# Interleaving row loads with DMA transposes on SyncE, with new scheduler estimates, in a fused attention and SwiGLU kernel

## The chip, the cores and the metric

The kernel runs on one core of a Trainium2 chip. The metric is device time in microseconds (us) of one execution. Each variant was run several times, and medians are given. One run of each was profiled. A span is the profiled execution from its first to its last instruction, some 2 us shorter than the run's time.

## The reference

```python
# q, k, v: (8, 8, 576, 64) batch, head, row, dim;  s: (8, 8, 576)
scores = q @ k.T / 8                       # causal
cum    = cumsum(max(s, 0))                 # decay along the rows
scores = where(causal, -1e9, scores + min(-(cum_i - cum_j), 0))
x      = softmax(scores) @ v               # -> (4608, 512), heads side by side
xn     = x / sqrt(mean(x * x) + 1e-6) * rms_g
out    = (silu(xn @ w_gate) * (xn @ w_val)) @ w_out     # 512 -> 1536 -> 512
```

## The kernel before

The 4608 rows of the feed-forward part are cut into nine chunks of 512. The attention of batch b+1 runs on TensorE in the gaps of chunk b's matmuls. For batches 2 to 7, SyncE's queue carries three kinds of work: 15 row loads of a batch (five each of k, q and v, 256 KB, the fifth of each half that), 15 DMA transposes (five each of K, Q and the normalised x), and 4 output writes per chunk.

The program gives every operation an engine, an estimated duration and a key. A list scheduler simulates the engines with these estimates and so fixes the order of each engine's instructions before anything runs. For SyncE it also holds back a transfer until the simulated transfers in flight are nearly done:

```python
# in Plan.schedule(): candidates e of an engine, r = earliest start
if o.dma and e == "sp":
    r = max(r, self.dma_free - 3.0)
...
begin = max(self.dma_free, s + o.us + o.lags[0])
self.dma_free = begin + o.dma
o.done = self.dma_free + o.lags[1]
```

The operations that the change touches (second argument of `dma_start`: SyncE's estimated issue time; `dma`: estimated transfer time; `lags`: estimated lead and landing time):

```python
def load_rows(dst, src, b, eng, key):
    for sc in range(NB):                                  # NB = 5 blocks of 128 rows
        n = 128 if sc < 4 else 64
        ops.append(I(eng, "dma_start", 0.88 if eng == "pool" else 0.4, key=key,
                     dma=1.28 * n / 128, lags=(1.2, 1.2 if b < 2 else 4.2), ...))

def prep_cast(b, which, key):                             # which: 0 = k, 1 = q
    for sc in range(NB):
        I("dve", "tensor_copy", 0.34, key=key + sc, out=dst[0:n, sc], in_=src[0:n, sc])
        I("sp", "dma_start_transpose", 1.27, key=key + sc, dma=0.65, lags=(0.5, 2.7), ...)

def ffn2(c, key, step):                                   # second matmul stage of a chunk
    for tb in range(4):
        ...                                               # 12 matmuls into one PSUM bank O
        o = nxt("osb", osb)                               # three buffers, in turn
        I("act", "activation", 0.6, ..., out=o, in_=O, func=AF.Copy, scale=0.5)
        I("sp", "dma_start", 0.4, key=key, dma=0.72, out=out[...], in_=o)
...
for c in range(NCH):                                      # chunk c, K = 36 * c
    ...                                                   # FFN1 of chunk c
    for w in range(2):
        prep_cast(b, w, K - 14)                           # b = c + 1
    ...
    n = b + 1                                             # loads of the batch after it
    for o in load_rows(k_nat, k, n, "sp", K + 16) + load_rows(q_nat, q, n, "sp", K + 16): ...
    lv = load_rows(v_nat[n % len(v_nat)], v, n, "sp", K + 16)
    ...
```

## Time and profile before

| | before |
|---|---|
| median of 4 runs | 376.86 us (375.39 to 378.92) |
| span of the profiled run | 373.1 us (a run of 374.8 us) |
| TensorE busy | 341.8 us, 92% |
| TensorE idle | 31.3 us |

The profile is cut from the last matmul of one chunk's second stage to that of the next. These are chunks 3 to 6 of the kernel before; the columns are start and end, length, busy time of each engine with its instructions, granted clock, DMA share and GB/s.

```profile
144.70:185.50 40.80, 37.96 (x352) 27.68 (x352) 30.62 (x56) 25.87 (x55) 15.46 (x24) 0.96 0.85 160
185.50:227.10 41.60, 36.77 (x253) 17.67 (x257) 28.72 (x56) 26.61 (x57) 14.22 (x23) 1.00 0.83 159
227.10:266.70 39.60, 36.62 (x252) 17.63 (x256) 29.26 (x55) 25.58 (x55) 14.07 (x21) 1.00 0.85 162
266.70:304.20 37.50, 36.43 (x253) 17.61 (x257) 23.98 (x48) 22.40 (x48) 8.11 (x16) 1.00 0.39 76
```

TensorE, the first busy column, needs 36.4 to 36.8 us of a chunk at full clock, and the chunks take up to 41.6.

### The profile page before, as it was taken

The page shows a single profiled execution, that of the slowest core. Times are in us where ns is not written, and L with a number is a line of the kernel's source. Part 1 is how long each engine was busy: PE and PEld are TensorE (multiplying, and loading weights), DVE is VectorE, ACT ScalarE, POOL GpSimd, SP SyncE. Part 2 cuts the span into 40 slices and gives each one's busy share as a digit, 9 for nine tenths or more (in the row PEclk, how much of TensorE's full clock was granted, in tenths as well). Part 3 has the DMA queues.
Part 4 walks back from the last instruction along what each step waited for, and adds up shares of the span by engine and source line. Part 5 has one row for each costly group of instructions (what it writes and reads, how often), then busy time and mean ns, then how long its engine had stood idle before and what let it go on. Part 6 is the DMA issues. An engine that isn't in the chain of part 4 may idle for free.

```text
span 373.1 us, 7766 instructions
## 1 busy us (share of the span) xinstructions
PE 341.8 (92%) x2907; PEld 207.6 (56%) x2934; DVE 251.6 (67%) x486; ACT 230.4 (62%) x469; POOL 127.8 (34%) x211
## 2 busy tenths in 40 slices
PE   3869999999999997999979799979999999999993
PEld 3558775788577864787435444444445444444441
DVE  6478946797937895588837893879388638806830
ACT  3959698888769825874767547863687533313321
POOL 8976452504361544134613370345123200000000
PEclk9999999999999999899999999999999999999999
DMA  8999997977985997699758986699650170020012
GB/s 125 215 226 208 193 184 164 162 176 153 200 192 116 190 179 132 179 156 198 133 128 183 198 151 115 167 203 174 114 148 2 30 149 0 0 87 29 0 43 78
DMA packets 138356, 51.13 MB, mean 137 GB/s; under 512 B 127300, under 2 KB 132936, under 8 KB 138312
## 3 DMA queue, kind: packets, MB, share of 16 engines
q1 hardware_dynamic: 131688, 41.13, 55.8%
q0 software_dynamic: 6624, 9.44, 14.4%
q8 instruction: 25, 0.41, 0.5%
q14 instruction: 19, 0.16, 0.2%
HBM read 38.16 MB, written 9.44 MB: 128 GB/s over the span
## 4 chain that ended last, share of the span: by engine, by line
PE 62%; DMA 12%; DVE 9%; POOL 5%; SPq 4%; ACT 3%; issue 3%; DVEq 0%; ACTq 0%; POOLq 0%
PE psc L373 9%; PE psb L373 8%; PE psd L373 8%; PE psg L373 8%; PE psh L373 7%; PE psa L373 7%; PE psf L373 7%; PE pse L373 6%; DMA v_nata<-in_v_dram 5%; SPq L356 4%; DVE Hs L356 2%; DMA QTb<-q_bf 2%; DMA out_dram<-osbb 2%; DMA q_nat<-in_q_dram 1%; DMA k_nat<-in_k_dram 1%
## 5 line engine op out<-in xcount | busy, mean ns | idle before, releaser
L373 PEld LDWEIGHTS <-wv_sb 128*128 128x128 bf16 x624 | 60.7, 98 | 39.5 <-issue 7.2
L373 PEld LDWEIGHTS <-wg_sb 128*128 128x128 bf16 x624 | 58.6, 98 | 32.5 <-issue 5.1
L373 PEld LDWEIGHTS <-Hs 128*128 128x128 bf16 x432 | 41.3, 98 | 49.9 <-DVE Hs L356 2.1
L356 POOL TENSOR_TENSOR vwb<-v_nata,wT 128x512 bf16<-128x512 f32 (+1 forms) x20 | 21.1, 1073 | 12.2 <-DMA v_nata<-in_v_dram 11.9
L356 POOL TENSOR_SCALAR_AFFINE_SELECT Ea<-Ea 128x512 bf16<-128x512 bf16 x8 | 5.1, 644 | 56.0 <-ACT Ea L356 56.0
L356 ACT ACTIVATE sq_scr<-x_blka 128x512 bf16<-128x512 bf16 x19 | 12.0, 632 | 15.9 <-DVE x_blka L356 15.6
L356 DVE CAST q_bf<-q_nat 128x512 bf16<-128x512 f32 (+1 forms) x30 | 18.4, 621 | 3.7 <-DMA q_nat<-in_q_dram 3.7
L373 PE MATMUL psf<-xnT,wv_sb 128*128 128x256 bf16 (+1 forms) x116 | 20.6, 313 | 0.2
L356 ACT ACTIVATE sq_scr<-x_blkb 128x512 bf16<-128x512 bf16 x20 | 12.6, 630 | 13.1 <-DVE x_blkb L356 12.6
L356 POOL TENSOR_TENSOR vwa<-v_nata,wT 128x512 bf16<-128x512 f32 (+1 forms) x15 | 16.2, 1094 | 9.5 <-DMA v_nata<-in_v_dram 9.3
L356 DVE CAST k_bf<-k_nat 128x512 bf16<-128x512 f32 (+1 forms) x30 | 15.1, 515 | 5.2 <-DMA k_nat<-in_k_dram 5.2
L373 PE MATMUL psc<-wout_sb,Hs 128*128 128x512 bf16 x69 | 17.0, 379 | 0.9 <-DVE Hs L356 0.7
L373 PE MATMUL psd<-xnT,wg_sb 128*128 128x256 bf16 (+1 forms) x95 | 17.5, 316 | 0.1
L373 PE MATMUL pse<-xnT,wg_sb 128*128 128x256 bf16 (+1 forms) x102 | 17.3, 304 | 0.1
L373 PE MATMUL psh<-wout_sb,Hs 128*128 128x512 bf16 x70 | 16.6, 379 | 0.5 <-DVE Hs L356 0.4
L373 PE MATMUL psg<-wout_sb,Hs 128*128 128x512 bf16 x70 | 16.6, 379 | 0.1
L356 ACT ACTIVATE sq_scr<-q_bf 128x1024 bf16<-128x1024 bf16 (+1 forms) x18 | 16.5, 916 | 0.2
L373 PE MATMUL psc<-xnT,wg_sb 128*128 128x256 bf16 (+1 forms) x83 | 14.9, 316 | 1.8 <-DVE xnT L356 1.5
L373 PE MATMUL psb<-xnT,wg_sb 128*128 128x256 bf16 (+1 forms) x95 | 16.3, 308 | 0.1
L356 ACT ACTIVATE sq_scr<-k_bf 128x1024 bf16<-128x1024 bf16 (+1 forms) x18 | 16.3, 908 | 0.0
L356 DVE SCALAR_TENSOR_TENSOR x_blkb<-x_blkb,alb,gB 128x512 bf16<-128x512 bf16 x15 | 12.1, 859 | 5.0 <-POOL alb L356 5.0
L373 PE MATMUL psa<-xnT,wv_sb 128*128 128x256 bf16 (+1 forms) x75 | 13.4, 311 | 1.9 <-DVE u_sbc L356 1.7
(456 smaller groups left out, 859.6 us busy)
## 6 DMA issues: line engine op xcount, KB each, us to landing
k_nat<-in_k_dram SPq DMA_DIRECT2D x24, 256.0 KB, 4.7
q_nat<-in_q_dram SPq DMA_DIRECT2D x24, 256.0 KB, 5.8
v_nata<-in_v_dram SPq DMA_DIRECT2D x24, 256.0 KB, 5.1
out_dram<-osba SPq DMA_DIRECT2D x12, 256.0 KB, 2.3
out_dram<-osbb SPq DMA_DIRECT2D x12, 256.0 KB, 2.4
out_dram<-osbc SPq DMA_DIRECT2D x12, 256.0 KB, 2.4
v_nata<-in_v_dram POOLq DMA_DIRECT2D x8, 256.0 KB, 11.0
wg_sb<-in_moe_w_gate_dram POOLq DMA_DIRECT2D x2, 768.0 KB, 12.9
```

The costliest lines, as they stand in the source:

```text
L356: o = R.add(eng, us, lambda: f(**{n: real(a) for n, a in kw.items()}), outs, ins, key=key, lat=LAT[eng], kind=kind, dma=dma, name=outs[0]. ...
L373: nc.tensor.matmul(out, lhsT=lhsT, rhs=rhs, start=st, stop=sp)
```

## The change

Its intent: row loads go between the transposes, block by block, as soon as a buffer row is free, so that data is on chip long before its cast. With it come new estimates for the scheduler, a new rule for holding SyncE's transfers back, and another order in batch 0. The diff, cut to its core:

```diff
+        sp_free = 0.0                                    # end of SyncE's own transfers
-                        r = max(r, self.dma_free - 3.0)
+                        r = max(r, sp_free - 2.0)
+                if e == "sp":
+                    sp_free = self.dma_free
...
+    def load_row(dst, src, b, sc, eng, key):             # one of the five rows
-   dma_start  0.4   dma=1.28 * n / 128   lags=(1.2, 1.2 if b < 2 else 4.2)
+   dma_start  0.45  dma=1.2 * n / 128    lags=(1.2, 1.2 if b < NRUN else MARGIN + 1.2)
...
-    def prep_cast(b, which, key):
+    def prep_cast(b, key):
         for sc in range(NB):
+            for src, dst, out in ((k_nat, k_bf, KT[b % 2]), (q_nat, q_bf, QT[b % 2])):
-   dma_start_transpose  1.27  lags=(0.5, 2.7)
+   dma_start_transpose  1.31  lags=(0.5, 0.9 + 0.6 * MARGIN)     # MARGIN = 3.0; x too
...
-            I("sp", "dma_start", 0.4, key=key, dma=0.72,         # output write
+            I("sp", "dma_start", 0.62, key=key, dma=0.75,
...
-            for o in load_rows(k_nat, ..., K + 16) + load_rows(q_nat, ..., K + 16):
-            lv = load_rows(v_nat[n % len(v_nat)], v, n, "sp", K + 16)
+            K2 = K - 14 + LEAD                                   # LEAD = 0.5
+            for sc in range(NB):
+                for dst, src in ((k_nat, k), (q_nat, q)):
+                    o = load_row(dst, src, n, sc, "sp", K2 + sc)
+            lv = [load_row(v_nat[...], v, n, sc, "sp", K2 + 6 + sc) for sc in range(NB)]
...
-                        prep_norm(b, w, i, K + 30)
+                        prep_norm(b, w, i, K + 20 + 2 * i)
... batch 0 ("the start"):
-            k2 = key + step * (HP * hf + HP + 1.5)
+            k2 = key + step * (HP * hf + HP + 1.5) - (3 if b == 0 and hf == 0 else 0)
-    vops = [prep_v(0, sc, "dve", -70) for sc in range(NB)]
+    vops = [prep_v(0, sc, "dve", -70 if sc < 2 else -62) for sc in range(NB)]
-    R.after(vops[2], norms[2])
+    R.after(vops[2], norms[3])
-    gp_ = small_bank()
+    gp_ = bank("g", 1)
```

Estimated transfer times of the loads issued by GpSimd become smaller as well (1.28 to 1.08 us, 4.0 to 3.95, 9.6 to 8.0, 8.9 to 7.8).

More of the change, by code (lines that the diff above doesn't have):

```diff
@@ L285 @@
     NRUN = 2
+    LEAD = 0.5
+    MARGIN = 3.0
     NTWO = 2
@@ L400, in load_runs @@
         p0 = KP * which
-        return I("pool", "dma_start", 0.8, key=key, dma=(4.0, 3.45)[b] * (h1 - h0) / 8, lags=(0.9, 1.3),
+        return I("pool", "dma_start", 0.8, key=key, dma=(3.95, 3.35)[b] * (h1 - h0) / 8, lags=(0.9, 1.3),
                  out=raw[b][p0 : p0 + KP, h0:h1, :, :].rearrange("p h c d -> p h (c d)"),
                  in_=(k, q)[which][b, h0:h1, :, :].rearrange("h (p c) d -> p h (c d)", c=KC))
-    def load_rows(dst, src, b, eng, key):
-        ops = []
-        for sc in range(NB):
-            n = 128 if sc < 4 else 64
-            ops.append(I(eng, "dma_start", 0.88 if eng == "pool" else 0.4, key=key,
-                         dma=1.28 * n / 128,
-                         lags=(1.2, 1.2 if b < 2 else 4.2),
-                         out=dst[0:n, sc], in_=src[b, :, sc * 128 : sc * 128 + n, :].rearrange(
-                             "h p d -> p h d")))
-        return ops
+    def load_row(dst, src, b, sc, eng, key):
+        n = 128 if sc < 4 else 64
+        return I(eng, "dma_start", 0.88 if eng == "pool" else 0.45, key=key, dma=(1.08 if eng == "pool" else 1.2) * n / 128,
+                 lags=(1.2, 1.2 if b < NRUN else MARGIN + 1.2), out=dst[0:n, sc],
+                 in_=src[b, :, sc * 128 : sc * 128 + n, :].rearrange("h p d -> p h d"))
+    def load_rows(dst, src, b, eng, key):
+        return [load_row(dst, src, b, sc, eng, key) for sc in range(NB)]
     def load_w(which, lo, hi, key):
         if which == 2:
-            return I("pool", "dma_start", 0.84, key=key, dma=9.6 * (hi - lo) / 12,
+            return I("pool", "dma_start", 0.84, key=key, dma=8.0 * (hi - lo) / 12,
                      out=wout_sb[:, lo:hi, :],
@@ L421, in load_w @@
         dst, src = ((wg_sb, moe_w_gate), (wv_sb, moe_w_val))[which]
-        return I("pool", "dma_start", 0.76, key=key, dma=8.9 * (hi - lo) / DF,
+        return I("pool", "dma_start", 0.76, key=key, dma=7.8 * (hi - lo) / DF,
                  out=dst[:, :, lo:hi],
@@ L438, in prep_transpose @@
             I("act", "activation", 0.57, key=key, out=o, in_=i, func=AF.Copy)
-    def prep_cast(b, which, key):
-        src, dst = ((k_nat, k_bf), (q_nat, q_bf))[which]
-        out = (KT, QT)[which][b % 2]
+    def prep_cast(b, key):
         for sc in range(NB):
             n = 128 if sc < 4 else 64
-            I("dve", "tensor_copy", 0.34, key=key + sc, out=dst[0:n, sc], in_=src[0:n, sc])
-            I("sp", "dma_start_transpose", 1.27, key=key + sc, dma=0.65, lags=(0.5, 2.7),
-              out=out[:, :, sc * 128 : sc * 128 + n], in_=dst[0:n, sc])
+            for src, dst, out in ((k_nat, k_bf, KT[b % 2]), (q_nat, q_bf, QT[b % 2])):
+                I("dve", "tensor_copy", 0.34, key=key + sc, out=dst[0:n, sc], in_=src[0:n, sc])
+                I("sp", "dma_start_transpose", 1.31, key=key + sc, dma=0.65,
+                  lags=(0.5, 0.9 + 0.6 * MARGIN),
+                  out=out[:, :, sc * 128 : sc * 128 + n], in_=dst[0:n, sc])
     def prep_norm(b, which, i, key):
@@ L613, in att_out @@
             c0 = b * S + tb * 128
-            I("sp", "dma_start_transpose", 1.27, key=key - 3, dma=0.65, lags=(0.5, 2.7),
+            I("sp", "dma_start_transpose", 1.31, key=key - 3, dma=0.65, lags=(0.5, 0.9 + 0.6 * MARGIN),
               out=xnT[:, :, c0 : c0 + 128 - p0], in_=x_blk[b % 2][p0:128, tb, :])
@@ L752 @@
             else:
-                for w in range(2):
-                    prep_cast(b, w, K - 14)
+                prep_cast(b, K - 14)
             if b < NRUN:
@@ L764 @@
             n = b + 1
-            for o in load_rows(k_nat, k, n, "sp", K + 16) + load_rows(q_nat, q, n, "sp", K + 16):
-                if n == NRUN:
-                    R.after(o, *vops)
-            lv = load_rows(v_nat[n % len(v_nat)], v, n, "sp", K + 16)
+            K2 = K - 14 + LEAD
+            for sc in range(NB):
+                for dst, src in ((k_nat, k), (q_nat, q)):
+                    o = load_row(dst, src, n, sc, "sp", K2 + sc)
+                    if n == NRUN:
+                        R.after(o, *vops)
+            lv = [load_row(v_nat[n % len(v_nat)], v, n, sc, "sp", K2 + 6 + sc) for sc in range(NB)]
             if n == NRUN:
```

## The prediction

> **What bounds the kernel now.** I read, in this order: the page's busy shares, then busy time by stretch, then SyncE's timeline, then the waits of TensorE and VectorE, then the first 30 us. The page says that TensorE is the engine to feed:
>
> ```profile
> PE 341.8 (92%) x2907; PEld 207.6 (56%) x2934; DVE 251.6 (67%) x486; ACT 230.4 (62%) x469; POOL 127.8 (34%) x211
> ```
>
> Of the 373.1 us span TensorE is idle for 31.3 us. 5.8 us of that lies before its first matmul and 5.1 us after its last (output and its landing); the change touches neither. What is left to win is 20.4 us. Where it lies, the stretches tell (length, then busy time of each engine, granted clock, DMA share, GB/s):
>
> ```profile
> core 0: us, PE busy (x) PEld busy (x) DVE busy (x) ACT busy (x) POOL busy (x), PEclk, DMA share, GB/s
> 120.00:160.00 40.00, 37.14 (x345) 26.86 (x344) 29.83 (x56) 26.30 (x57) 15.73 (x24) 0.96 0.86 162
> 160.00:199.60 39.60, 37.33 (x314) 23.28 (x315) 30.01 (x57) 26.22 (x56) 15.10 (x24) 1.00 0.87 160
> 199.60:239.20 39.60, 36.37 (x251) 17.55 (x255) 28.46 (x55) 25.42 (x54) 14.17 (x23) 1.00 0.86 162
> 239.20:279.00 39.80, 36.30 (x250) 17.35 (x253) 29.22 (x57) 25.57 (x55) 14.07 (x21) 1.00 0.84 161
> 64.00:120.00 56.00, 55.05 (x526) 41.30 (x527) 40.79 (x85) 44.46 (x95) 20.98 (x32) 1.00 0.84 171
> ```
>
> The four stretches from 120 to 279 us are one chunk of the feed-forward part each, with one batch of attention in it. TensorE idles 2.86 + 2.27 + 3.23 + 3.50 = 11.86 us in them, 7.5%. From 64 to 120 us, with the same kinds of work, it idles 0.95 us, 1.7%. Something holds the later chunks at 39.6 us. SyncE's timeline of one of them names it (start, time, what):
>
> ```profile
> 199.57 4.39 SPq L356 DMA_DIRECT2D k_nat<-in_k_dram  x5
> 204.01 6.49 SPq L356 DMA_DIRECT2D q_nat<-in_q_dram  x5
> 210.60 5.59 SPq L356 DMA_DIRECT2D v_nata<-in_v_dram  x5
> 216.28 2.57 SPq L356 DMA_TRANSPOSE xnT<-x_blkb  x2
> 218.94 1.22 SPq L356 DMA_TRANSPOSE KTa<-k_bf  x1
> ...
> 237.89 1.24 SPq L356 DMA_TRANSPOSE QTa<-q_bf  x1
> ```
>
> One piece begins where the last ended, from 199.57 to 239.18 us, where the next chunk's loads begin. Summed by kind over that chunk: 15 row loads 4.39 + 6.49 + 5.59 = 16.5 us, 15 transposes 18.6 us, 4 output writes 3.0 us; 38.0 us in all, and some 20 gaps make up the other 1.6 us. SyncE's queue is full, and its order is the pace of these chunks. The first load of a burst takes 0.57 us to issue, one in its middle 1.12 us: with several in flight SyncE is held to the rate at which they move. What TensorE feels of it:
>
> ```profile
> 149.27 0.27 PE L373 MATMUL psb<-QTa,KTa 64*128 64x256 bf16 x1 [2.21 <-DMA QTa<-q_bf]
> 189.48 0.27 PE L373 MATMUL psf<-QTb,KTb 64*128 64x256 bf16 x1 [1.62 <-DMA QTb<-q_bf]
> 209.73 0.66 DVE L356 CAST q_bf<-q_nat 128x512 bf16<-128x512 f32 x1 [1.51 <-DMA q_nat<-in_q_dram]
> 211.03 1.02 PE L373 MATMUL psa<-xnT,wv_sb 128*128 128x512 bf16 x4 [1.74 <-DVE u_sbc L356]
> ```
>
> Twice the scores wait for a transpose that came late. And VectorE, in order, sits before a cast whose q rows have not landed; the u product behind it in its queue is what TensorE then waits for (again at 250.93 us, 1.75 us). After the 2.21 us wait the clock fell as well:
>
> ```profile
> 144.00:152.00 8.00, 5.43 (x43) 3.56 (x41) 2.01 (x3) 2.84 (x6) 1.11 (x1) 0.91 0.59 131
> 152.00:160.00 8.00, 8.00 (x77) 6.51 (x76) 6.41 (x13) 7.45 (x18) 1.91 (x3) 0.88 0.59 158
> ```
>
> A mean of 0.91 and 0.88 over 8 us each is (0.09 + 0.12) x 8 = 1.7 us of clock lost, which counts as busy time. The start, last:
>
> ```profile
> 18.13 1.29 DVE L356 TENSOR_TENSOR vwa<-v_nata,psc 128x512 bf16<-128x512 f32 x2 [1.79 <-DMA v_nata<-in_v_dram]
> 20.62 0.43 PE L373 MATMUL psd<-vwa,Ee 128*128 128x65 bf16 x5 [2.30 <-DVE vwa L356]
> 26.15 1.03 PE L373 MATMUL psc<-xnT,wg_sb 128*128 128x256 bf16 x8 [1.51 <-DVE xnT L356]
> ```
>
> VectorE waits 1.79 us for v rows before it norms the last two head pairs of batch 0's first half, and the first feed-forward matmul starts at 26.15 us.
>
> **What the Trainium skill says.** "DMA: Bandwidth & Descriptors", section "Anatomy of one DMA": the DMA engines do not wait for semaphores; the wait is on the issuing sequencer. The timeline agrees: SyncE's issue order decides what starts, and a held issue holds all behind it. The same page, "Queues, rings and completion order": descriptors of one queue's ring are taken in order. So a transpose behind loads starts after them; here the first transpose after the v loads took 3.66 us from issue to landing against a median of 2.5 us. "TensorE: Matmul & The Clock Gate", Part 1: the clock is halved after an idle window of about 3.4 us. This trace fits only in part: 1.7 us lost is 3.4 us at half clock, but the wait before it was 2.2 us.
>
> **The change, part by part.** The instruction orders of both kernels were compared engine by engine. No operation is added or removed: TensorE has the same 1440 blocks of 512 columns of feed-forward work and the same attention work. What changes is order; the new durations and lags are only the scheduler's estimates.
>
> (1) Row loads. Before, SyncE issues 15 loads of a batch in a burst, shortly before that batch's casts and transposes. After, each pair of K and Q transposes of batch b is followed by the K and Q load of the same block of batch b+1, in the buffer rows that the casts have just freed; v loads come last in the chunk. So loads are almost a chunk ahead of their casts: the waits of VectorE on k and q rows and of GpSimd on v rows (21 us in all, 9 times) should go. Cost on SyncE: 15 transposes 18.6 us and 4 writes 2.5 us as before; 10 interleaved loads. A group of two transposes and two loads issues in 2 x 1.3 + 2 x 0.6 = 3.8 us; as an estimate from landing spacings (about 1.15 us for a load in a burst, 0.75 us for a transpose) it moves for 3.8 us. That is balanced, so a load will still be held at times: I take 0.75 us, 7.5 us for ten; the five v loads stay a burst, 5.6 us; gaps 1.6 us. Sum 18.6 + 2.5 + 7.5 + 5.6 + 1.6 = 35.8 us, where 39.6 us were needed. TensorE's 36.3 to 37.3 us become the longer of the two.
>
> (2) Places of the scores. In TensorE's order, counted in feed-forward blocks of 0.216 us, the first scores of batch 4 move from block 440 to 452, of batch 5 from 584 to 620, of batch 6 from 728 to 744; batch 7 stays at 872. Behind the third transpose pair they have 36 to 44 blocks, 7.8 to 9.5 us, against 2.6 us issue and 2.5 to 4 us landing. So the 2.21 and 1.62 us waits should go, and with the first the lost clock.
>
> Gain in the four chunks: 11.86 us idle + 1.7 us clock = 13.6 us at most. I keep 2.5% idle of 159 us, 4.0 us (1.7% is the rate of 64 to 120 us; some more because SyncE is at 35.8 us, and the wait of the second matmul stage for the last Hs, 0.4 to 0.7 us a chunk, does not depend on the loads). 13.6 - 4.0 = 9.6 us.
>
> (3) Batch 0. In VectorE's new order the v factors of blocks 3 and 4 still stand before the norms of pairs 2 and 3; only block 2's, 0.68 us, goes behind them and behind a square of 0.69 us. TensorE's transposes of x move ahead of half of the second half's matmuls. So the 1.79 us wait stays, and the second half starts later, at about 21.9 us for 20.62. The first feed-forward matmul should come at about 25.4 us, 0.7 us earlier. But batch 1's transposes now stand behind 52 feed-forward blocks for 60: TensorE reaches them at about 25.4 + 52 x 0.216 + 1.2 = 37.8 us, and q's first half landed at 39.7 us. A new wait of 1 to 2 us takes back the 0.7 us. Net 0, give or take 1.
>
> Sum: 377.0 - 9.6 + 0 = 367.4, say 367.5 us.
>
> **The rivals.** (A) SyncE stays the bound: if interleaved loads keep the 1.1 us of a burst, SyncE needs 18.6 + 2.5 + 11 + 5.6 + 1.6 = 39.3 us, and only the waits for q rows and the lost clock go, because data comes a chunk earlier: 371 to 374 us. For it speaks a DMA share of already 0.85, against it the 0.57 us of an issue with room. (B) Transposes stuck behind two loads in the ring land 1 to 2 us later, and scores wait for QT again, each with a chance of a halved clock: 370 to 375 us. For it speaks 3.66 us after a burst; against it the moved scores. (C) All idle time in the chunks falls to 1.7% or less and the start keeps its 0.7 us: 377.0 - 13.6 + 2.7 - 0.7 = 365.4; 362 if also the handovers inside chunks shrink. (D) Denser attention stretches (batch 5 in 78 blocks, before 88) make VectorE the bound there: some 1 us a chunk, 369 to 371 us.
>
> **Range and chances.** The 2% line is 369.5 us, so the middle lies only 2 us beyond it. C and the main line give faster (0.68); A, B and D, alone, mostly end between 369.5 and 375 (0.29); slower needs stalls that the old order did not have (0.03). Range 362 to 373 us.
>
> **What would show each step right or wrong.** Right: in SyncE's timeline loads of about 0.6 to 0.8 us between transposes, with waits for its producers; chunks of 37 to 38 us between 120 and 279 us; no wait of VectorE on k or q rows after 100 us, none of GpSimd on v rows; no scores waiting for QT over 1 us; clock 1.00 all through; first feed-forward matmul near 25.4 us and a wait for batch 1's q rows near 38 us. Wrong: chunks still near 39 us with SyncE without gaps (A), or waits of TensorE on QT (B) or on u and Hs products (D) in place of the old ones.

## The result

The changed kernel takes 360.71 us (median of 4 runs, 359.86 to 364.39) where the one before takes 376.86. The ratio is 0.9586, 95% interval 0.9507 to 0.9666: faster by 4.1%. A ratio here is the mean time of one kernel's fast runs over the mean time of the other's in the same rounds, so it is not quite the ratio of the medians. The prediction had said 367.5 us within 362 to 373: the direction was right, the size was not, and the result lies 1.3 us below the range. A later repeat gave 360.37 us, ratio 0.9592 (0.9547 to 0.9637).

The page's busy shares and the engines of the chain that ended last, of the changed kernel:

```profile
PE 339.0 (94%) x2934; PEld 206.7 (58%) x2934; DVE 247.0 (69%) x486; ACT 231.6 (65%) x469; POOL 126.5 (35%) x211
PE 78%; DMA 9%; POOL 6%; DVE 3%; issue 1%; ACT 1%; DVEq 0%; POOLq 0%; ACTq 0%
```

TensorE does the same work in 339.0 us (341.8 before), and idles 19.9 us of the span of 358.9, not 31.3. Before, TensorE had 62% of the chain and SyncE's queue 4%; SyncE has now left the list. Where the time went, chunk by chunk (lengths between the last matmuls of the second stages, in us; chunk 0 from the first feed-forward matmul on, which starts at 26.15 before and at 25.21 after):

| chunk | 0 | 1 | 2 | 3 | 4 | 5 | 6 | 7 | 8 |
|---|---|---|---|---|---|---|---|---|---|
| before | 42.3 | 38.1 | 38.2 | 40.8 | 41.5 | 39.7 | 37.4 | 31.5 | 31.1 |
| after | 43.2 | 37.5 | 38.1 | 36.1 | 36.1 | 37.7 | 35.9 | 31.5 | 31.1 |

The span shrank by 14.2 us, of which 4.7 + 5.4 + 2.0 + 1.5 = 13.6 us lie in chunks 3 to 6. (Medians differ by 16.1 us because the profiled run of before was 2.1 us below its median.) The same stretches of the changed kernel:

```profile
144.00:180.20 36.20, 36.20 (x354) 27.15 (x353) 29.79 (x61) 27.41 (x57) 13.75 (x23) 1.00 0.94 176
180.20:216.20 36.00, 35.99 (x257) 17.61 (x256) 26.38 (x50) 24.07 (x51) 14.62 (x23) 1.00 0.93 171
216.20:254.00 37.80, 36.39 (x258) 17.86 (x257) 29.91 (x58) 27.89 (x60) 13.91 (x22) 1.00 0.87 160
254.00:289.90 35.90, 35.90 (x258) 17.56 (x257) 23.84 (x48) 23.22 (x48) 8.12 (x16) 1.00 0.29 55
```

In three of the four TensorE has no idle time at all: 36.20 of 36.20, 35.99 of 36.00, 35.90 of 35.90. In chunk 5 it idles 1.4 us, in pieces of 0.2 to 0.7 us, each behind VectorE or GpSimd; none of these waits is on a transfer.

SyncE's timeline of the changed kernel (start, time, what), from the v loads of one chunk on:

```profile
159.38 4.98 SPq L361 DMA_DIRECT2D v_nata<-in_v_dram  x5
164.46 2.57 SPq L361 DMA_TRANSPOSE xnT<-x_blka  x2
167.12 1.98 SPq L361 DMA_TRANSPOSE KTb<-k_bf  x1
169.15 1.26 SPq L361 DMA_TRANSPOSE QTb<-q_bf  x1
170.46 0.58 SPq L361 DMA_DIRECT2D k_nat<-in_k_dram  x1
171.09 0.57 SPq L361 DMA_DIRECT2D q_nat<-in_q_dram  x1
171.76 1.49 SPq L361 DMA_TRANSPOSE KTb<-k_bf  x1
...
175.90 0.91 SPq L361 DMA_DIRECT2D out_dram<-osba  x1
```

The loads do sit in pairs between transposes, at 0.57 to 0.64 us each. But the queue is as full as ever. The next chunk's v loads start at 196.19, 36.81 us later. The pieces between are k and q loads 5.9 us, v loads 5.0, transposes 21.9, output writes 2.2, and gaps 1.9. The transposes cost 3.3 us more than before, because several are held where others take 1.2 to 1.3 us: three right behind a pair of loads (1.49, 1.54 and 1.67 us), one behind the v loads and two transposes (1.98), and two of x behind output writes (1.65 and 1.74).

One thing I had overlooked shows in the waits of ScalarE: who waited, for what, us in total, times, longest. Before:

```profile
ACT osbc L356 <- DMA out_dram<-osbc: 8.0, 2, 5.2
ACT osbb L356 <- DMA out_dram<-osbb: 5.0, 2, 2.6
ACT osba L356 <- DMA out_dram<-osba: 3.2, 1, 3.2
```

And after, the only such line of any output buffer:

```profile
ACT osbb L361 <- DMA out_dram<-osbb: 1.7, 1, 1.7
```

Before, an output write was issued late because it stood in SyncE's full queue: in chunks 2 to 5, 4 to 12 us after ScalarE had filled its buffer (ends of the copies set against the issues in the timeline). With three buffers, ScalarE then waited before the fourth copy of each of the chunks 1 to 5, 16.2 us in all, and held a PSUM bank meanwhile. TensorE itself waited for these copies only 0.5 us in all. After, writes of the same chunks are issued within 0 to 4 us.

The start: the wait behind the v factors is still there, as the prediction said.

```profile
21.52 0.31 PE L378 MATMUL psd<-vwa,Ee 128*128 128x65 bf16 x5 [2.52 <-DVE vwa L361]
```

### The profile page after: what moved, and what is told of

The parts are those of the page before. It is cut to its first block, busy times and chain, and to the rows that moved or that the text cites. A ratio compares the mean times of both kernels' runs of the same rounds, so it can differ in the third digit from the quotient of the medians.

```text
span 358.9 us, 7827 instructions
## 1 busy us (share of the span) xinstructions
PE 339.0 (94%) x2934; PEld 206.7 (58%) x2934; DVE 247.0 (69%) x486; ACT 231.6 (65%) x469; POOL 126.5 (35%) x211
## 4 chain that ended last, share of the span: by engine, by line
PE 78%; DMA 9%; POOL 6%; DVE 3%; issue 1%; ACT 1%; DVEq 0%; POOLq 0%; ACTq 0%
PE pse L378 12%; PE psa L378 10%; PE psh L378 10%; PE psb L378 10%; PE psf L378 9%; PE psd L378 9%; PE psc L378 9%; PE psg L378 8%; DMA wv_sb<-in_moe_w_val_dram 5%; DMA v_nata<-in_v_dram 4%; POOL v_nata L361 2%; POOL q_nat L361 1%; ACT sq_scr L361 1%; DVE Hs L361 1%; POOL Ee L361 1%
## 5 line engine op out<-in xcount | busy, mean ns | idle before, releaser
L378 PE MATMUL pse<-wout_sb,Hs 128*128 128x512 bf16 x96 | 22.5, 379 | 0.0
L361 ACT ACTIVATE sq_scr<-x_blka 128x512 bf16<-128x512 bf16 x19 | 12.0, 630 | 12.0 <-DVE x_blka L361 11.6
L378 PE MATMUL psc<-xnT,wg_sb 128*128 128x256 bf16 (+1 forms) x104 | 18.8, 316 | 0.0
L361 DVE SCALAR_TENSOR_TENSOR x_blkb<-x_blkb,alb,gB 128x512 bf16<-128x512 bf16 x15 | 11.0, 779 | 10.8 <-POOL alb L361 10.7
L378 PE MATMUL psa<-wout_sb,Hs 128*128 128x512 bf16 x72 | 17.0, 379 | 0.0
L378 PE MATMUL psb<-xnT,wv_sb 128*128 128x256 bf16 (+1 forms) x100 | 16.5, 302 | 0.2 <-DVE u_sbc L361 0.2
L361 DVE CAST q_bf<-q_nat 128x512 bf16<-128x512 f32 (+1 forms) x30 | 15.3, 510 | 0.9 <-ACT sq_scr L361 0.9
L378 PE MATMUL pse<-xnT,wg_sb 128*128 128x256 bf16 (+1 forms) x92 | 15.5, 305 | 0.0
L378 PE MATMUL psa<-xnT,wg_sb 128*128 128x256 bf16 (+1 forms) x84 | 15.5, 318 | 0.0
L361 POOL TENSOR_TENSOR vwa<-v_nata,wT 128x512 bf16<-128x512 f32 (+1 forms) x15 | 15.1, 1039 | 0.0
L361 DVE CAST k_bf<-k_nat 128x512 bf16<-128x512 f32 (+1 forms) x30 | 13.7, 456 | 0.0
```

The lines of the kernel that those rows point to most:

```text
L361: o = R.add(eng, us, lambda: f(**{n: real(a) for n, a in kw.items()}), outs, ins, key=key, lat=LAT[eng], kind=kind, dma=dma, name=outs[0]. ...
L378: nc.tensor.matmul(out, lhsT=lhsT, rhs=rhs, start=st, stop=sp)
```

## The experiments

All kernels gave correct results, and all 18 runs were timed in rounds with the kernel before on the same chip. The texts on record number the theories in the order in which they were formed: the first two credit the interleaving, the third the scheduler's new estimates, the fourth the late output writes alone, the last the pace of SyncE's issues.

### First set: the parts of the change, one at a time

**Interleaving alone.** The new load order and paired casts, with all old estimates and the old start:

```diff
-   load_rows(k_nat, ..., K + 16) + load_rows(q_nat, ..., K + 16);  v the same
+   load_row per block at K - 14 + 0.5 + sc;  v at K - 14 + 6.5 + sc
    (every duration, transfer time, lag and the hold-back rule as before)
```

> The kernel before with one part of the change: K and Q row loads of batch b+1 follow the two transposes of the same block of batch b, v loads last, casts of k and q alternate. The scheduler's estimates and the start of batch 0 stay as before. Theory 1 (SyncE's issue time is the pace of chunks 3 to 6, because a burst of loads is held to the rate of the transfers) and theory 2 (rows land too late for the in-order VectorE and GpSimd) both expect nearly all of the gain: about 363 us, chunks 3 to 6 near 36 to 37 us each. Theory 3 (the gain comes from later places of the scores in TensorE's order, set by the new lags) expects 373 us or more, with scores waiting for QT.

Measured: 382.03 us, ratio 1.0139 (1.0062 to 1.0216). It is slower than the kernel before. The waits for Q transposes and q rows are gone, just as planned, but TensorE now waits for ScalarE's copies, up to 6.26 us, and its mean granted clock falls to 0.976 (0.995 before). One such place, from the timelines of SyncE, ScalarE and TensorE of this kernel:

```profile
231.69 3.94 SPq L357 DMA_DIRECT2D v_nata<-in_v_dram  x4
235.72 1.10 SPq L357 DMA_DIRECT2D out_dram<-osbb  x1
240.14 0.60 ACT L357 ACTIVATE osbb<-psa 128x512 f32<-128x512 f32 x1 [8.59 <-DMA out_dram<-osbb]
240.79 1.86 PE L374 MATMUL psa<-xnT,wv_sb 128*128 128x512 bf16 x4 [6.26 <-ACT osbb L357]
```

The buffer osbb had been filled by 225.04 us, but SyncE gets to its write only at 235.72, behind k, q and four v loads. ScalarE waits 8.59 us to reuse the buffer, and TensorE 6.26 us for the PSUM bank that ScalarE could not empty. So the interleaving by itself relieves one wait and makes another, and the two theories that credit it alone, with 363 us, fall. The third had the time right (373 us or more) and the reason wrong: no scores wait for QT.

**New estimates alone.** Loads stay in a burst and the start stays old; all new issue and transfer times, the hold-back rule and the earlier key of the norms are in.

```diff
-   r = max(r, self.dma_free - 3.0)
+   r = max(r, sp_free - 2.0)
    (and 0.4 -> 0.45, 0.4 -> 0.62, 1.27 -> 1.31, MARGIN, prep_norm at K + 20 + 2 * i)
```

> The kernel before with only the scheduler's new durations, lags, load throttle and the earlier key of the norm squares; loads stay a burst of 15 behind the transposes, the start of batch 0 as before. Theories 1 and 2 expect within 1.5% of before: 371 to 379 us, with SyncE's queue still full at about 39 us a chunk. Theory 3 expects most of the gain, about 363 us.

Measured: 369.39 us, 0.9776 (0.9711 to 0.9841), about half of the gain, and between what the first two theories and the third expected. TensorE still waits 6.4 us for Q and K transposes and ScalarE 13.9 us for output writes.

**The start alone.**

```diff
-    R.after(vops[2], norms[2])
+    R.after(vops[2], norms[3])        (and the other three edits of batch 0)
```

> The kernel before with only the changes of batch 0: v factors of blocks 2 to 4 at a later key, block 2's after the fourth norm, the first half's squares and outputs 3 earlier, the small transposes of g in a bank group of its own. All theories expect the same as before, 375 to 378 us: the first feed-forward matmul 0.5 to 1 us earlier, and that lost again by the end of chunk 0, whose end in the two known profiles is 68.5 and 68.4 us.

Measured: 375.82 us, 0.9987 (0.9920 to 1.0054): nothing. The first feed-forward matmul comes at 25.00 us, 1.15 us earlier, yet chunk 0 ends at 68.7 us for 68.5.

**Everything but the start.**

```diff
-    R.after(vops[2], norms[3])
+    R.after(vops[2], norms[2])        (and the other three edits undone)
```

> The changed kernel without the changes of batch 0. All theories expect the time of the changed kernel within 1 us: 360 to 362 us.

Measured: 363.28 us, 0.9623 (0.9567 to 0.9679), 1.3 us above the expected range; the third set comes back to this.

Without the start, the four corners are 377.4 us (neither), 382.0 (interleaving), 369.4 (estimates) and 363.3 (both). Added up, the two single effects make +4.7 - 8.0 = -3.3 us; together they make -14.1. The other 10.8 us come only from having both.

### Second set: which estimates, and are the late writes the cause

**Interleaving plus SyncE's new issue and transfer times.** The hold-back rule is in too; the norms' key, GpSimd's estimates and the start stay old. Since the lags are the same in both kernels, the expectation's other branch could not come true; this kernel differs from "everything but the start" in the norms' key and GpSimd's estimates alone.

```diff
     on top of "interleaving alone":
-   r = max(r, self.dma_free - 3.0);  0.4 / 1.28 (load), 1.27 (transpose), 0.4 / 0.72 (write)
+   r = max(r, sp_free - 2.0);        0.45 / 1.2,        1.31,             0.62 / 0.75
```

> Interleaved loads alone (382.0 us) plus only the new issue and transfer costs on SyncE and the new load throttle; lags, key of the norm squares and batch 0 as before. In its order the output writes stand before the loads that stood before them in the run with interleaved loads alone. Theory 4 expects that to bring most of the fall: 362 to 367 us. If the added lags are what counts, it stays above 372 us.

Measured: 363.98 us, 0.9678 (0.9633 to 0.9723). A handful of constants takes the interleaved kernel from 382 to 364 us, nearly level with "everything but the start". ScalarE's waits for output writes fall from 21.9 to 0.7 us. SyncE's timeline shows where the writes now stand:

```profile
215.28 0.58 SPq L360 DMA_DIRECT2D q_nat<-in_q_dram  x1
215.96 0.83 SPq L360 DMA_DIRECT2D out_dram<-osbb  x1
216.88 0.38 SPq L360 DMA_DIRECT2D out_dram<-osbc  x1
```

They follow a pair of loads directly, 3 to 4 us after their copies started (211.80 and 213.89 us), with no v loads in between.

**The changed kernel with no slack in its landing lags.**

```diff
-    MARGIN = 3.0
+    MARGIN = 0.0
```

> The changed kernel with the added lag (3 us for loads, 1.8 us for transposes in the scheduler's estimate) set to 0, so scores and casts are placed closer behind their transfers. If the added slack is what the new estimates bring, it loses 4 us or more, with TensorE waiting for QT. If the issue costs and the load throttle are what they bring (so that SyncE's order of writes, loads and transposes fits the chip), it stays within 2 us of the changed kernel, 359 to 363 us.

Measured: 361.79 us, 0.9599 (0.9562 to 0.9637). The slack for late landings hardly matters.

**Output writes issued by ScalarE**, in the kernel before and in "interleaving alone", to take them out of SyncE's queue:

```diff
-            I("sp", "dma_start", 0.4, ..., out=out[...], in_=o)
+            ... nc.scalar.dma_start(out=out[...], in_=o)      (order as planned for SyncE)
```

> The kernel before with the output writes issued from ScalarE's queue; all other instructions keep their order. It takes about 3 us a chunk from SyncE's queue of 38 us. Theory 1 (SyncE's queue is the pace of chunks 3 to 6) expects 1.5 to 3 us a chunk, 366 to 371 us. Theory 3 (only places of scores) and theory 2 (rows late) expect less: rows are issued no earlier relative to their casts than SyncE's order allows, so 373 us or more if SyncE's total is not what counts.

> The kernel with interleaved loads alone (382.0 us), with the output writes issued from ScalarE's queue in place of SyncE's; every engine's other instructions keep their order. Theory 4, formed from that run's trace: interleaving does take the waits for rows and for QT away, but under the old estimates SyncE's order puts the output writes behind K, Q and v loads for which SyncE in fact needs longer, the three output buffers are not free, ScalarE cannot evacuate and TensorE stops (6.3, 3.8, 2.9 and 1.2 us, some with a halved clock after). It expects a fall of 14 us or more, to 362 to 368 us. If interleaving as such is slow (transposes and loads disturbing one another in the DMA queues), it stays above 376 us.

Measured: 387.01 us, 1.0279 (1.0238 to 1.0320), and 382.25 us, 1.0134 (1.0079 to 1.0189). These two are no test. ScalarE's queue then waited for transfers of SyncE's, as the waits of the second kernel show:

```profile
ACT osbb L357 <- DMA xnT<-x_blkb: 8.6, 1, 8.6
```

An output write from ScalarE stood behind the landing of a transpose issued by SyncE. No data connects the two, but a semaphore does. In the packed trace this write and that transpose signal their landing on the same semaphore (115), and the write waits for it: it is issued at 236.54 us, 0.02 us after the transpose landed. In this kernel 10 of the 36 writes, and 11 of 36 in the other, are issued within 0.1 us of the landing of the transfer of SyncE's that last used their semaphore. So the writes left SyncE's queue but not its order, and ScalarE was blocked besides.

### Third set: a fourth output buffer, and the start once more

If late writes hurt only through the three buffers, a fourth frees ScalarE without touching SyncE.

```diff
-    NOSB = 3
+    NOSB = 4
```

In the kernel before:

> The kernel before with four output buffers in place of three, the loads in bursts as before. The scheduler moves SyncE's output writes by a few places; TensorE's order from batch 4 on is the same as before. Theory 4 (an output write late in SyncE's queue holds an output buffer, so ScalarE cannot evacuate the last of a chunk's four blocks) says that the 19.1 us that ScalarE waited for writes fall to under 4 us, and part of the gain comes with it: 368 to 374 us; SyncE's queue (theory 1) keeps the rest. If late writes do not count, 375 us or more.

Measured: 378.50 us, 1.0036 (0.9993 to 1.0079). ScalarE's waits for writes fall from 16.2 us to none, but TensorE's waits for Q and K transposes rise from 4.1 to 8.4 us. Nothing is gained, and theory 4's 368 to 374 us did not come. (The expectation's 19.1 us count in a wait of 2.9 us at 359.4 us, in the last chunk, which the changed kernel has too, there for TensorE.)

In "interleaving alone":

> Interleaved loads alone (382.0 us) with four output buffers in place of three; TensorE's order from batch 4 on is the same as with three. The run with the writes on ScalarE's queue was no test of theory 4: there the writes still waited for transposes of SyncE's queue. Here nothing changes queue. Theory 4 expects TensorE's waits for osb (6.3, 3.8, 2.9, 1.2 us) and the clock lost after them to go: 361 to 368 us. If interleaving under the old estimates costs by itself, it stays above 375 us.

Measured: 379.36 us, 1.0055 (1.0010 to 1.0101). The waits for ScalarE's copies go as theory 4 said, but not the time, and this comes in their place on TensorE:

```profile
241.21 0.51 PE L374 MATMUL psg<-vwa,Ea 128*128 128x65 bf16 x6 [4.74 <-POOL Ea L357]
```

GpSimd, in order, has its mask behind products that wait for v rows, which come late in SyncE's queue. So the late writes alone are not the cause: free one customer of SyncE's queue, and the next one in it waits.

**The changed kernel and the one without the start, with five rounds each:**

```diff
     (the two kernels as they are)
```

> The changed kernel again, on the same chip as the next run: 359 to 362 us.

> The changed kernel without the changes of batch 0, again, beside it. In the first round it stood 0.4% of before (1.4 us) behind the changed kernel, within the intervals. If the start is worth its earlier first feed-forward matmul (25.2 for 26.8 us in the profiles), it is 1 to 2.5 us slower than the changed kernel; if nothing, the intervals overlap and the medians lie within 0.7 us.

Measured: 360.37 us (0.9592, 0.9547 to 0.9637) and 363.26 us (0.9639, 0.9607 to 0.9672). The start is worth 2.9 us by the medians, 2.1 us by the means (two of the changed kernel's six runs took over 363 us) and 0.5% by the ratios; the intervals just overlap. In the profiles, the first feed-forward matmul comes 1.7 us later without the start (26.72 and 25.05 us), and chunk 1 is 0.7 us longer.

### Fourth set: is SyncE the pace

**v loads of batches 2 to 7 issued by GpSimd**, each engine's order otherwise as planned. That takes some 5 us of issues a chunk off SyncE.

```diff
             lv = ...
+            for sc, w in enumerate(lv):
+                w.fn = lambda ...: nc.gpsimd.dma_start(out=v_nat[0][0:n_, sc], in_=v[...])
```

In the kernel before:

> The kernel before with the v row loads of batches 2 to 7 issued from GpSimd's queue; the scheduler still plans them on SyncE, so every other instruction of every engine keeps its place, SyncE has 5 loads (5.6 us) less a chunk, and bytes and results stay. Theory 1 again, in the form of the runs so far (SyncE falls behind the static plan, and whatever depends on it, writes, QT or v rows, is late; freeing one of them shows the next): chunks 3 to 6 fall from 40.8, 41.5, 39.7 and 37.4 us to 36 to 38 us each, 363 to 368 us. If the places in TensorE's order or the traffic of the DMA engines are the bound, it stays above 373 us.

Measured: 369.63 us, 0.9803 (0.9761 to 0.9844). Seven us come from five issues a chunk less on SyncE, with every other place in the order kept; that the v rows also come at other times is part of the edit. It is less than expected. Three of the four chunks do fall to 35.9 to 37.0 us; the fourth takes 43.9, with one wait of 3.28 us for VectorE up to 209.09 us and a granted clock of 0.60 over 8 us. Behind it stands a load:

```profile
207.36 1.09 DVE L356 CAST q_bf<-q_nat 128x512 bf16<-128x512 f32 x1 [2.62 <-DMA q_nat<-in_q_dram]
```

Beside GpSimd's v loads, these q loads took 7.4 to 11.1 us from issue to landing, where the same burst of the kernel before took 4.9 to 6.2.

In "interleaving alone":

> Interleaved loads alone (382.0 us) with the v row loads of batches 2 to 7 issued from GpSimd's queue, all else in its place. Theory 1: SyncE's lateness at the output writes (9 to 15 us behind the evacuation) falls to a few us, TensorE's waits for osb and for Ea go: 361 to 367 us. If interleaving itself slows transfers, above 375 us.

Measured: 374.66 us, 0.9928 (0.9874 to 0.9982); a fourth run, 388.78, was slow. It too gains some 7 us on its base of 382, far from the expected 361 to 367, and keeps two large waits, 5.66 us for a Q transpose and 4.17 us for a copy by ScalarE.

**Each output write as two of 64 rows**, the plan unchanged. By the traces this adds 3.0 us of issues a chunk (45.4 us for 18.2 over the 36 writes before, 44.5 for 17.5 in the changed kernel); the bytes stay the same.

```diff
-            I("sp", "dma_start", ..., out=out[128 rows], in_=o)
+            w.fn = lambda ...: [nc.sync.dma_start(out=out[r0 + r : r0 + r + 64, :], in_=o[r : r + 64, :])
+                                for r in range(0, 128, 64)]
```

In the kernel before:

> The kernel before with each output write issued as two of 64 rows; nothing else moves. Theory 1: SyncE, full at 38 of 39.6 us, gets 1.6 to 2 us more a chunk, and the time grows by 5 to 8 us, to 382 to 385 us. If SyncE is not the pace: within 2 us of before.

Measured: 394.37 us, 1.0446 (1.0396 to 1.0496); 17.6 us above the kernel before in the same rounds, more than twice what was expected.

In the changed kernel:

> The changed kernel with each output write issued as two of 64 rows; nothing else moves. SyncE gets 4 more issues of 0.4 to 0.5 us a chunk, 1.6 to 2 us. If the change gave SyncE real room, the time grows by under 2 us (360 to 363 us). If SyncE is still the pace, by 5 to 8 us in chunks 3 to 6.

Measured: 374.05 us, 0.9934 (0.9871 to 0.9996); 13.7 us above the median of the changed kernel's five rounds, again about twice what was expected. One line of its SyncE timeline:

```profile
185.29 1.19 SPq L686 DMA_DIRECT2D out_dram<-osbb  x2
```

A half costs 0.6 us, no less than most wholes (0.33 to 0.98 us). Chunks 2 to 6 grow by 3.8, 1.5, 2.2, 2.1 and 2.0 us: of some 15 us of issues added there 11.6 arrive, 1.7 of them as lost clock after a wait in chunk 2. That a split write also holds its buffer longer is not what costs: TensorE waits 4.3 us for Q transposes and 0.3 us for a copy. So SyncE in the changed kernel has next to no room: it has been made to fit, not freed.

### Fifth set: can the changed kernel be improved the same way

**The changed kernel, with v loads issued by GpSimd.**

```diff
+                w.fn = lambda ...: nc.gpsimd.dma_start(...)     (v loads of batches 2 to 7)
```

> The changed kernel, with the v row loads of batches 2 to 7 issued from GpSimd's queue and the plan's own order unchanged. It takes about 5 us of issue time per chunk off SyncE, of 36.8. Theory 6 (SyncE's issue time is still the pace in the changed kernel, together with TensorE): the chunk of 37.7 us falls to TensorE's own 36.0 to 36.4, the others by at most 0.3, so 358 to 360 us against 360.4. Rival (TensorE alone sets the pace now, SyncE has slack): no change, 360.0 to 361. If the loads, freed, take transfer time from the transposes: above 361.

Measured: 364.54 us (five fast runs; the sixth, 370.28, was slow), 0.9670 (0.9613 to 0.9726). This is slower than the changed kernel's 360.4. Chunks 3 to 6 take 36.1, 36.4, 38.3 and 35.9 us, as in the changed kernel, although SyncE now stands idle at times (3.7, 5.5 and 5.9 us). So my expectation that chunk 5 would shrink failed: it idles 2.1 us, 1.7 of them behind VectorE. The rival holds for chunks 3, 4 and 6, where TensorE idles at most 0.15 us and sets the pace alone. The loss lies in chunk 2, 43.9 us for 38.1:

```profile
133.64 0.42 DVE L361 CAST q_bf<-q_nat 64x512 bf16<-64x512 f32 x1 [4.42 <-DMA q_nat<-in_q_dram]
136.03 2.53 PE L378 MATMUL pse<-wout_sb,Hs 128*128 128x512 bf16 x8 [3.41 <-DVE u_sba L361]
```

The u product stands behind that cast in VectorE's queue. The cast's q rows were issued at 123.69 us, among GpSimd's five v loads (122.6 to 126.9 us), and landed 9.8 us later; in the changed kernel the same load took 3.7 us. So the expectation's third branch came true, for a load in place of a transpose. The two 43.9 us chunks, this one and that of the kernel before with the same edit, have the same cause: q rows that landed late beside GpSimd's v loads. After TensorE's wait the granted clock was 0.86 over 12.1 us.

**The changed kernel, with a fourth output buffer.**

```diff
-    NOSB = 3
+    NOSB = 4
```

> The changed kernel with a fourth output buffer. ScalarE waited 1.7 us for output writes in the changed kernel, and TensorE has nearly no wait left after 130 us. Theory 6 and its rival: no change, within 1 us of 360.4. A theory by which the output writes still cost time: 357 to 359.

Measured: 360.57 us, 0.9573 (0.9526 to 0.9620): no different from the changed kernel. Late writes cost nothing more there. No version tried beats the changed kernel.

## Why the prediction was wrong in size

The theory that the runs support: before, SyncE's in-order queue sets the pace of chunks 3 to 6. The old estimates let the scheduler place transfers as if SyncE could issue them faster than it does, so whatever stands behind them comes late. Interleaving and truer estimates together give an order in which every transfer is in time although the queue is still full; then TensorE's 36 us a chunk are the bound. That SyncE's queue held these chunks, and that the gain needs both parts of the change, is shown by the runs. That the new estimates work because they are truer is argued: the old ones add up to 26.7 us of issues a chunk and the new ones to 28.9, where the traces have 38.0 and 36.8. Why so small a step puts the transfers in time, no run shows.

- **What bounds the kernel: right, with a gap.** SyncE was the pace: 5 us fewer issues gained 7 us in all, and split writes cost 17.6. But I read only the waits on loads and transposes, and missed the output writes in the same queue, although ScalarE's waits for them (16.2 us in all, of which 0.5 us reached TensorE) stood in the profile. Of the waits that part (1) wanted to remove, the 21 us are GpSimd's alone; VectorE's, 8.9 us in 12, come on top. From batch 2 on both are gone.
- **"What changes is order; the new durations and lags are only the scheduler's estimates": the step that failed.** Lags aside, which do not change, the sentence is literally true, and I concluded from it that the estimates were a detail and credited the whole gain to the interleaving. Interleaving alone is slower than before (382.0 us), and the estimates take it to 364.0. Order was the cost, and the estimates make the order. Which of the constants matters most, the issue times, the transfer times or the hold-back rule, was not separated.
- **Part (1), SyncE's sum of 35.8 us: a term mis-sized.** Loads took less than assumed (0.57 to 0.64 us for 0.75), but transposes took 21.9 us for the 18.6 assumed, because several are held. The sum came to 36.8 us, nearly as long as TensorE's chunk, and the split writes show that no room is left.
- **Part (2), Q transposes in time: right.** No scores wait for them in the changed kernel, and the clock lost at 149 us is not lost.
- **"I keep 2.5% idle of 159 us, 4.0 us": the mis-sized term of the sum.** I took the idle rate of earlier chunks and added to it because I expected SyncE to stay close. Measured, chunks 3 to 6 keep 145.9 - 144.5 = 1.4 us, all of it in one chunk. The gain there was 13.6 us, where I had written 9.6. Of these 4.0 us, 2.6 are the idle time that I kept too much of. The rest was no term of my sum: TensorE's busy time in these chunks, lost clock apart, fell from 146.1 to 144.5 us for the same work, and no run shows why. Together that is 4.0 us of the 6.8 by which the prediction missed. Another 2.1 us is that I took a gain, worked out from a profiled run of 374.8 us, off a median of 377.0; the profile can't tell what that run had not to wait for.
- **Part (3), the start: right on what happens, wrong on its net of 0.** First feed-forward matmul 25.21 us (25.4 predicted), second half at 21.52 (21.9). The wait for batch 1's q rows near 38 us did not come. The start was worth nothing in the kernel before, presumably because the queue decides later anyway, and 2 to 3 us in the changed one. Without it, chunk 2 of the new order ends at 146.0 us, later than the 144.7 of before; with it, at 144.0. Over chunks 0 to 2 the whole change thus gained 0.7 us, the rest of the miss. The clock was not 1.00 all through: 0.89 and 0.90 from 16 to 32 us, again 1.7 us lost; in the profiled repeat of the changed kernel nothing was lost there.
- **The rivals.** A had the right picture of a full queue and the wrong conclusion: full is not late. B's late transposes came (3.7 to 3.8 us to landing behind a pair of loads in the chunk shown, for 2.5), but the scores had room. D's denser attention did not bind: VectorE is busy at most 29.9 us a chunk. C, all idle time gone and the start kept, said 365.4, or 362 with shorter handovers; it was nearest, and I gave it too little weight.
- **A count.** The 1440 blocks of 512 columns are 1296 by the trace (480 matmuls of 512 columns and 768 of 256 in the first stages, 432 of 512 in the second). No sum rests on it.

Left open: which constant does it and why, why loads beside GpSimd's take up to 11 us, and writes from ScalarE with semaphores of their own.

## What to carry to other kernels

Where a static scheduler fixes the order, its cost estimates are part of the kernel: check them against issue times in the trace, and treat a changed constant in a diff as a change of order; work out first whether it changes at all. When one in-order queue is full, sum its issues and look at everything in it, since freeing one customer only lets the next one wait. To find whether a queue sets the pace, add a known amount to it and take a known amount away.

## What the Trainium skill lacked or had wrong

- "DMA: Bandwidth & Descriptors", section "Issuing engines are not separate DMA queues", says that spreading DMAs over engines only saves the issuing sequencer's time, "which is usually small relative to the DMA itself". Of a single load that holds here too (k loads before, from 140 us on: 0.57 to 1.32 us of issue; median to landing, of all, 4.7 us). Summed over one queue it did not: 38.0 us of issues in a chunk of 39.6 were the pace, and moving five loads a chunk to GpSimd took the kernel before from 376.7 to 369.6 us.
- The same page, section "Rules for kernel authors", advises against splitting a transfer by partitions because the halves share the engines. The runs agree and add a price that the section lacks: each half costs 0.6 us of issue, no less than most wholes, and the 36 splits of a run cost 13.7 us in one kernel and 17.6 in the other.
- None of the pages read says how long an issue is held behind others. Here a transpose of 128 rows by 512 held SyncE for 1.2 to 1.3 us as a rule, and in the changed kernel for 1.3 to 2.3 us (median 1.5) right behind a load. A load's own issue took 0.57 to 0.64 us with room and 1.12 us in the middle of a burst.
- None of them says that issuing from another engine need not decouple a transfer: in a program that gives one landing semaphore to transfers of both queues in turn, 10 or 11 of 36 output writes from ScalarE waited for transfers of SyncE's, mostly transposes, on which they did not depend, and ScalarE with them, once for 8.6 us.
- "TensorE: Matmul & The Clock Gate", Part 1, names an idle window of about 3.4 us before the clock halves. Waits of 2.21 us (before) and 2.52 us (the start of the changed kernel) each came with 1.7 us of lost clock; one of 2.30 us at the start of the kernel before did not, nor did one of 3.03 us in the profiled repeat of the changed kernel.
